# Regrouping the attention bursts inside a fused attention and SwiGLU kernel

## The chip, the core and the metric

One core of one Trainium2 chip runs the whole program. The metric is device microseconds of an execution; a profiled execution also gives a span, from its first to its last instruction, and the clock that TensorE was granted.

## The reference

Attention over 8 batches of 8 heads (576 positions, head width 64) with a band of 32 positions to each side and 8 global positions, followed by a SwiGLU feed-forward block over the 4608 tokens.

```python
scores = scale * np.matmul(q, k.transpose(0, 1, 3, 2))
mask = np.abs(pos[:, None] - pos[None, :]) <= window          # window = 32
mask = mask | is_global[:, None] | is_global[None, :]
attn = softmax(np.where(mask, scores, -1e9))
x = np.matmul(attn, v).transpose(0, 2, 1, 3).reshape(4608, 512)
g = x @ w_gate                                                # 512 x 1536
out = (g * sigmoid(g) * (x @ w_val)) @ w_out                  # 1536 x 512
```

## The kernel before

**The outer order.** The feed-forward block works on chunks of 512 tokens (`ffn`), nine of them. A chunk is 16 units: twelve gate units (`gate`, four matmuls for `pg` and four for `pv`, all 128x512, lines 754 and 784 to 793) and four output units (`outp`, twelve matmuls each, line 815). The attention of batch b is cut into steps, and the steps are put into the gaps after the units by hand: `gaps[n]` lists what follows unit n, and batch b from 2 on has the base `16 * (b - 1)`, so that it is computed during chunk b-1. Below, "gap 7" of a batch is the gap after unit 7 of that chunk. Every engine runs its instructions in program order; only waits between engines are put in by the framework.

**What a chunk needs.** Chunk c starts at token 512c, batch b at token 576b. Chunk 2 so needs the first 384 rows of batch 2, that is the outputs of `step_AV(0)`, `step_AV(1)` and `step_AV(2)`, transposed into `xT`.

**The steps of a batch from 2 on.** `step_GT` transposes the global rows. `step_S2` and `step_SG` give the scores of the two global parts (lines 444 and 422); their exponentials run on ScalarE, their masks on VectorE. `step_P2T` transposes the global weights, by TensorE for batches 2 and 3 and by a DMA on the SP queue from batch 4 on. `step_S(u)`, u from 0 to 4, gives the band scores (line 510; sixteen matmuls of 64x64, eight for u = 4), then an exponential on ScalarE (line 518) and the band mask on VectorE (line 524). `step_AV2` multiplies the global weights by the values (line 479), and three VectorE instructions turn that into `gvt` (lines 486 to 494). `step_AV(tp)`, tp from 0 to 3, and `step_AV8` add up the outputs (lines 563, 572, 591, 599) and normalise them on VectorE (lines 539 to 545). `step_X(tp)` and `step_X8` bring them into `xT` by a transposing DMA on SP.

**Buffers in PSUM.** Pool `psc` has one tile of two banks, pool `pm` another one of two banks, and pool `pf` has four single banks, which hold the `pg` and `pv` of two gate units, or an output unit's `po`. In batches 2 to 7, `step_S2`, all `step_S` and `step_AV8` use `psc`; `step_GT`, `step_SG`, `step_AV2` and all `step_AV` use `pm`.

**Loads.** Queries and keys of batches 2 to 7 are cast into DRAM by POOL's DMAs (`kf`, `qf`, line 109) and read from there by transposing DMAs on SP into `kT` and `qT` (lines 116 and 120, `tr_at`).

**The tiling of TensorE.** Profile rows carry the shape in which the array is used: gate and output matmuls and transposes 128\*128, `step_S` and the first matmuls of `step_AV` (line 563) 64\*128, `step_S2`, `step_SG` and `step_AV2` 128\*32, the other matmuls of `step_AV` and `step_AV8` 128\*64, the first two of `step_AV8` 64\*64.

Of the kernel before, what the change touches and what calls it, by code (L numbers as in the profile page):

```python
# [17 lines left out]
P = 128  # L18
# [8 lines left out]
def kernel(  # L27
# [322 lines left out]
    def attention(b):  # L350
# [122 lines left out]
            nc.scalar.copy(out=st["p2t"], in_=ps)  # L473

        def step_AV2():
            ps = mtile([P, 2, W], FP32, "ps_av2")
            for u in range(5):
                for hp in range(HP):
                    nc.tensor.matmul(  # L479
                        out=ps[32 * hp : 32 * hp + 32, :, :],  # L480
                        lhsT=st["p2t"][:, u, 32 * hp : 32 * hp + 32],
                        rhs=va[:, u, 2 * hp : 2 * hp + 2, :],
                        start=(u == 0), stop=(u == 4), skip_group_check=True,
                    )
            gv = bp.tile([P, 2, 2, W], BF16, tag="gv", name="gvt")
            nc.vector.tensor_tensor(
                out=gv, in0=bc(ps, [[0, 2], [W, 2], [1, W]]),
                in1=bc(dmh, [[2, 2], [1, 2], [0, W]]), op=ALU.mult,
            )
            lo = work.tile([P, 2, 2], FP32, tag="lo", name="lo")  # L490
            nc.vector.tensor_tensor(
                out=lo, in0=bc(ps[:, :, D : D + 1], [[0, 2], [W, 2]]), in1=dmh, op=ALU.mult
            )
            nc.vector.tensor_tensor(
                out=gv[:, :, :, D + 1], in0=lo, in1=gv[:, :, :, D], op=ALU.subtract
            )
            st["gv"] = gv

        def step_S(u):
            hg, t0 = ((0, 0), (1, 0), (0, 4), (1, 4), (None, 8))[u]  # L500
            pool, tag = (pm, "m") if (b == 0 and u in (2, 3)) or (b == 1 and u == 4) else (psc, "sc")
            ps = pool.tile([P, 2, 512], FP32, tag=tag, name="ps_s")
            if hg is None:
                slots = [(hp, hp, 8) for hp in range(HP)]
            else:
                slots = [(4 * i + tl, 2 * hg + i, t0 + tl) for i in range(2) for tl in range(4)]
            for slot, hp, t in slots:
                for par in range(2):
                    r = 64 * par
                    nc.tensor.matmul(  # L510
                        out=ps[:, par, 64 * slot : 64 * slot + 64],
                        lhsT=kT[r : r + 64, hp, 64 * t : 64 * t + P],
                        rhs=qTs[b][r : r + 64, hp, 64 * t : 64 * t + 64],
                        start=True, stop=True,
                    )
            ns = len(slots)
            pe = ppool.tile([P, 2, ns, 64], BF16, tag="pe", name="pe", bufs=3)
            nc.scalar.activation(  # L518
                out=pe, in_=ps[:, :, 0 : 64 * ns].rearrange("p r (s c) -> p r s c", c=64),
                func=AF.Exp, scale=SCALE,  # L520
            )
            pt = ppool.tile([P, 2, ns, 64], BF16, tag="p", name="pt")
            st["p", u] = pt
            mult = lambda: nc.vector.tensor_tensor(  # L524
                out=pt.rearrange("p r s c -> p (r s) c"),
                in0=pe.rearrange("p r s c -> p (r s) c"),
                in1=bc(band, [[0, 2 * ns], [1, 64]]), op=ALU.mult,
            )
            if b == 0:
                st["p*", u] = mult  # L530
            else:
                mult()
# [18 lines left out]
        def step_AV(tp):  # L551
            st["xa", tp] = work.tile([P, H, D], BF16, tag="xa", name="xa", bufs=4)
            if b == 0:
                pool, tag = (pm, "m") if tp % 2 else (psc, "sc")
            elif b < XQ:
                pool, tag = (psc, "sc") if tp == 2 else (pm, "m")
            else:
                pool, tag = pm, "m"
            full = pool.tile([P, 2, 512], FP32, tag=tag, name="ps_av")
            ps = full[:, :, 0 : 4 * W].rearrange("p g (h c) -> p g h c", c=W)  # L560
            for hg in range(2):
                r = slice(64 * hg, 64 * hg + 64)
                nc.tensor.matmul(  # L563
                    out=ps[:, hg], lhsT=st["pg"][r, P * tp : P * tp + P],
                    rhs=st["gv"][r].rearrange("p h r c -> p (h r) c"),
                    start=True, stop=False, skip_group_check=True,
                )
            for hg in range(2):
                pt = st["p", 2 * (tp // 2) + hg]
                for hl in range(4):  # L570
                    for e in range(2):
                        nc.tensor.matmul(  # L572
                            out=ps[64 * e : 64 * e + 64, hg, hl, :],
                            lhsT=pt[:, hl % 2, 4 * (hl // 2) + 2 * (tp % 2) + e, :],
                            rhs=(va if e == 0 else st["vb"])[:, tp, 4 * hg + hl, :],
                            start=False, stop=(hl == 3), skip_group_check=True,
                        )
            if b == 0:
                st["xa*", tp] = lambda: normalise(ps, st["xa", tp], 8)
            else:  # L580
                normalise(ps, st["xa", tp], 8)
# [87 lines left out]
        def vb():  # L669
            st["vb"] = load_vb(b)  # L670

        def vb0(t):
            st["vb"] = load_vb(0)
            nc.vector.tensor_copy(out=st["vb"][0:64, 0:2], in_=va[64:128, 0:2])
            nc.vector.tensor_copy(out=st["vb"][64:128, 0:2], in_=va[0:64, 1:3])
            nc.scalar.copy(out=st["vb"][0:64, 2:4], in_=va[64:128, 2:4])
            nc.scalar.copy(out=st["vb"][64:128, 2:4], in_=va[0:64, 3:5])

        L = lambda f, *a: (lambda: f(*a))
        if b == 0:  # L680
            act, dve = nc.scalar.copy, nc.vector.tensor_copy

            M = lambda *key: (lambda: st[key if len(key) > 1 else key[0]]())
            def kqm0():
                gather_mask(0, *g0, eng=nc.vector)

            return [
                L(squares), L(tables_a),
                L(step_T0, "k", 0, act), L(step_T0, "k", 1, act),
                L(step_T0, "q", 0, act), L(step_T0, "q", 1, dve), L(tables_b),  # L690
                L(step_S, 0), L(step_T0, "k", 2, dve), L(step_S, 2), L(step_T0, "k", 3, act),
                kqm0, L(step_T0, "q", 2, act), L(step_GT), L(step_T0, "q", 3, dve),
                L(step_S2), L(step_SG), M("p*", 0), M("p2*"), M("pg*"),
                L(step_S, 1), L(step_P2T), L(step_S, 3), L(warm, 1),
                M("p*", 1), L(vb0, 0), L(step_AV2), L(warm, 2), M("p*", 2),
                L(step_AV, 0), M("xa*", 0), L(step_AV, 1), L(warm, 1), M("p*", 3), L(step_X, 0),
                L(step_AV, 2), L(warm, 1), M("xa*", 1), M("xa*", 2), L(step_X, 1),
                L(step_AV, 3), M("xa*", 3),
            ], [L(step_X, 2)], [L(step_X, 3)], [L(step_S, 4), M("p*", 4)], [L(step_AV8)], [L(step_X8)]
# [17 lines left out]
        if b < XQ:  # L717
# [6 lines left out]
                14: [L(step_S, 4), L(step_AV, 3), L(step_X, 3)],  # L724
                15: [L(step_AV8)], 16: [L(step_X8)],
            }
        return {
            1: [L(step_GT), vb],
            2: [L(step_S2), L(step_SG)] + ([L(step_P2T)] if b >= XP else []),
            4: [L(step_S, 0)] + ([] if b >= XP else [L(step_P2T)]),  # L730
            7: [L(step_S, 1), L(step_AV2)],
            9: [L(step_S, 2), L(step_AV, 0), L(step_X, 0)],
            11: [L(step_S, 3), L(step_AV, 1), L(step_X, 1)],
            12: [L(step_S, 4), L(step_AV, 2), L(step_X, 2)],
            14: [L(step_AV, 3), L(step_AV8), L(step_X, 3), L(step_X8)],
        }

# [101 lines left out]
    part(1, 2 * P, 3 * P)  # L839
    part(0, 3 * P, CH)  # L840
    part(1, 3 * P, CH)
    gaps = {i: [] for i in range(9)}
    for i, g in enumerate([s4, av8, x8]):
        gaps[(0, 3, 6)[i]] += g
    def at(n, f, *a):
        gaps.setdefault(n, []).append(lambda: f(*a))

# [18 lines left out]
    for b in range(XQ, B):  # L866
        o = 16 * (b - 1)
        for i, g in attention(b).items():
            if b == 2 and i < 4:
                i += 1  # L870
            gaps[o + i] = gaps.get(o + i, []) + g
        if b > 3:
            tr_at[b] = o - 16 + 5
        if b > 4:
            cast_at[b] = o - 32 + 8
        if b > 2:
            v_at[b] = o - 16 + 2
            if b % 2 == 0:
                g_at[b] = o - 16 + 6
                m_at[b] = o - 16 + 13  # L880
# [43 lines left out]
```

The softmax here doesn't subtract the row's maximum and nothing guards it: scores larger than these inputs give would overflow.

## Time and profile before

| | |
|---|---|
| time | 360.15 us median of 3 runs (359.66 to 360.69) |
| span of the profiled execution | 361.1 us, mean granted clock 0.991 |
| TensorE matmul | 343.2 us busy, 95% |
| VectorE, ScalarE, GpSimd | 232.5, 151.2, 91.8 us busy |
| gate matmuls (line 754) | 107.1 + 107.5 us |
| output matmuls (line 815) | 92.4 us |
| band scores (line 510) | 16.2 us |
| output of attention (line 572) | 14.7 + 14.7 us |

Busy times of TensorE overlap, because matmuls are pipelined: what one costs is the distance from its start to the start of the next. A wait is charged to the engine that stood idle and named after what ended last before it resumed. Idle time of an engine other than the one that sets the end costs nothing by itself.

### The profile page before, as it was taken

What the parts mean: (1) busy time and instruction counts of PE and PEld (TensorE: products, weight loads), DVE (VectorE), ACT (ScalarE), POOL (GpSimd) and SP (SyncE); (2) the same over time, 40 slices, a digit from 0 to 9 for tenths busy, and PEclk for the clock granted to TensorE, in tenths of its full rate; (3) what the DMA queues carried; (4) which work ended last, traced back from release to release, by engine and by line L of the source; (5) the groups of instructions that cost most, each with busy time, mean ns of one, the idle gap of its engine ahead of it and who ended that gap; (6) DMA issues with size and microseconds to landing.
All of it is one profiled execution on the core that took longest, in us unless ns stands there. A gap on an engine that the chain in (4) does not pass through costs nothing.

```text
span 361.1 us, 7611 instructions
## 1 busy us (share of the span) xinstructions
PE 343.2 (95%) x3079; PEld 168.9 (47%) x3131; DVE 232.5 (64%) x468; ACT 151.2 (42%) x231; POOL 91.8 (25%) x110
## 2 busy tenths in 40 slices
PE   2989999999979999999999999999999999999996
PEld 2565554444434444444444444444444444444444
DVE  6777784388715893688458854886388727814750
ACT  5745762455313552354235532553254323323322
POOL 7964754805145111600183011000000000000000
PEclk9989999999998999999999999999999999999999
DMA  7999999999999998998989989622330230011002
GB/s 107 145 205 204 184 207 156 124 249 158 156 176 199 140 154 125 130 206 129 120 151 156 165 101 148 148 55 61 100 104 2 58 96 30 2 58 59 2 15 102
DMA packets 153539, 44.14 MB, mean 122 GB/s; under 512 B 140064, under 2 KB 148000, under 8 KB 153504
## 3 DMA queue, kind: packets, MB, share of 16 engines
q0 software_dynamic: 101216, 19.14, 67.1%
q1 hardware_dynamic: 52288, 24.51, 34.2%
q8 instruction: 24, 0.39, 0.5%
q14 instruction: 11, 0.09, 0.1%
HBM read 38.02 MB, written 16.52 MB: 151 GB/s over the span
## 4 chain that ended last, share of the span: by engine, by line
PE 84%; DMA 7%; DVE 3%; ACT 2%; issue 2%; POOL 1%; another core or an unknown queue 1%; SPq 0%; POOLq 0%; DVEq 0%
PE pg L754 24%; PE pv L754 23%; PE po L815 22%; PE ps_s L510 3%; PE ps_av L572 3%; DMA xT<-xa 2%; DMA p2t<-p 2%; DMA k_bf<-in_k_dram 2%; PE ps_av L563 1%; ACT pe L518 1%; PE ps_s L444 1%; DVE pt L524 1%; PE po L802 1%; PE ps_av L479 1%; PE ps_t L367 1%
## 5 line engine op out<-in xcount | busy, mean ns | idle before, releaser
L754 PE MATMUL pg<-xT,wg_sb 128*128 128x512 bf16 x399 | 107.1, 382 | 4.4 <-DMA xT<-xa 2.5
L754 PE MATMUL pv<-xT,wv_sb 128*128 128x512 bf16 x413 | 107.5, 382 | 0.2
L787 DVE SCALAR_TENSOR_TENSOR gv<-th,pg 128x512 bf16<-128x512 bf16 x107 | 73.4, 686 | 49.9 <-ACT th L785 49.1
L785 ACT ACTIVATE th<-pg 128x512 bf16<-128x512 f32 x107 | 63.9, 598 | 85.7 <-PE pg L754 82.9
L815 PE MATMUL po<-wo_sb,h 128*128 128x512 bf16 x399 | 92.4, 380 | 0.7
L791 DVE TENSOR_TENSOR h<-gv,pv 128x512 bf16<-128x512 bf16 x107 | 73.6, 688 | 11.8 <-PE pg L754 0.5
L754 PEld LDWEIGHTS <-wv_sb 128*128 128x128 bf16 x424 | 41.7, 98 | 50.7 <-issue 1.1
L754 PEld LDWEIGHTS <-wg_sb 128*128 128x128 bf16 x424 | 38.7, 98 | 47.0 <-issue 5.7
L815 PEld LDWEIGHTS <-h 128*128 128x128 bf16 x420 | 39.4, 98 | 45.2
L102 POOL DMA_DIRECT2D va<-in_v_dram x40 | 34.9, 976 | 91.8 <-PE ps_av L572 81.5
L820 ACT ACTIVATE osb<-po 128x512 f32<-128x512 f32 x35 | 20.9, 597 | 81.7 <-PE po L815 57.7
L518 ACT ACTIVATE pe<-ps_s 128x1024 bf16<-128x1024 f32 (+1 forms) x40 | 37.5, 938 | 17.8 <-PE ps_s L510 17.8
L524 DVE TENSOR_TENSOR pt<-pe,band 128x1024 bf16<-128x1024 bf16 (+1 forms) x40 | 25.5, 636 | 15.8 <-ACT pe L518 15.8
L545 DVE TENSOR_TENSOR xa<-ps_av,den 128x512 bf16<-128x512 f32 (+1 forms) x40 | 25.5, 638 | 1.4
L539 DVE TENSOR_REDUCE den<-ps_av 128x8 f32<-128x16 f32 (+1 forms) x40 | 6.7, 167 | 30.1 <-PE ps_av L572 27.8
L510 PEld LDWEIGHTS <-kT 64*128 64x128 bf16 x576 | 11.4, 98 | 15.9 <-issue 15.1
L109 POOL DMA_DIRECT2D kf<-in_k_dram x6 | 13.4, 2234 | 18.3 <-issue 12.6
L510 PE MATMUL ps_s<-qT,kT 64*128 64x64 bf16 x576 | 16.2, 196 | 0.1
L109 POOL DMA_DIRECT2D qf<-in_q_dram x6 | 16.0, 2659 | 1.3 <-DMA qf<-in_q_dram 1.3
L572 PE MATMUL ps_av<-vb,pt 128*64 128x66 bf16 x256 | 14.7, 201 | 0.0
L572 PE MATMUL ps_av<-va,pt 128*64 128x66 bf16 x256 | 14.7, 201 | 0.0
L572 PEld LDWEIGHTS <-pt 128*64 128x64 bf16 x512 | 11.1, 113 | 4.4 <-issue 0.5
(138 smaller groups left out, 190.2 us busy)
## 6 DMA issues: line engine op xcount, KB each, us to landing
out_dram<-osb SPq DMA_DIRECT2D x35, 256.0 KB, 2.2
vb<-va SPq DMA_DIRECT2D x14, 264.0 KB, 6.6
kf<-in_k_dram POOLq DMA_DIRECT2D x6, 576.0 KB, 17.6
qf<-in_q_dram POOLq DMA_DIRECT2D x6, 576.0 KB, 19.9
va<-in_v_dram POOLq DMA_DIRECT2D x24, 128.0 KB, 8.5
va<-in_v_dram POOLq DMA_DIRECT2D x16, 96.0 KB, 8.3
wg_sb<-in_moe_w_gate_dram POOLq DMA_DIRECT2D x3, 512.0 KB, 10.3
wv_sb<-in_moe_w_val_dram POOLq DMA_DIRECT2D x3, 512.0 KB, 12.3
```

The lines of the kernel that those rows point to most:

```text
L102: nc.gpsimd.dma_start(out=va[lo:hi, u, :, 0:D], in_=vs[t0 + lo : t0 + hi])
L109: nc.gpsimd.dma_start(out=t, in_=src[b].rearrange("h s d -> s h d"))
L510: nc.tensor.matmul(out=ps[:, par, 64 * slot : 64 * slot + 64], lhsT=kT[r : r + 64, hp, 64 * t : 64 * t + P], rhs=qTs[b][r : r + 64, hp, 64 ...
L518: nc.scalar.activation(out=pe, in_=ps[:, :, 0 : 64 * ns].rearrange("p r (s c) -> p r s c", c=64), func=AF.Exp, scale=SCALE,)
L524: mult = lambda: nc.vector.tensor_tensor(out=pt.rearrange("p r s c -> p (r s) c"), in0=pe.rearrange("p r s c -> p (r s) c"), in1=bc(band, ...
L545: nc.vector.tensor_tensor(out=xa.rearrange("p (g h) d -> p g h d", g=g), in0=bc(ps, pst + [[1, D]]), in1=bc(den, [[4, g], [1, 4], [0, D]]) ...
L572: nc.tensor.matmul(out=ps[64 * e : 64 * e + 64, hg, hl, :], lhsT=pt[:, hl % 2, 4 * (hl // 2) + 2 * (tp % 2) + e, :], rhs=(va if e == 0 els ...
L754: nc.tensor.matmul(out=ps[:, 0:n], lhsT=w[:, cc, P * fc : P * (fc + 1)], rhs=xT[:, cc, t0 : t0 + n], start=(cc == 0), stop=(cc == NCC - 1),)
L785: nc.scalar.activation(out=th[:, 0:n], in_=pg[:, 0:n], func=AF.Tanh, scale=0.5)
L787: nc.vector.scalar_tensor_tensor(out=gv[:, 0:n], in0=th[:, 0:n], scalar=1.0, in1=pg[:, 0:n], op0=ALU.add, op1=ALU.mult,)
L791: nc.vector.tensor_tensor(out=st["h"][:, fc, 0:n], in0=gv[:, 0:n], in1=pv[:, 0:n], op=ALU.mult)
L815: nc.tensor.matmul(out=po, lhsT=st["h"][:, fc, P * ts : P * (ts + 1)], rhs=wo_sb[:, fc, :], start=(fc == 0), stop=(fc == NFC - 1),)
```

## The change

For batches 3 to 7, `step_S(0)` and `step_S(1)` follow one another after unit 4, with `step_S(1)` and `step_S(2)` in `pm` instead of `psc`. `step_S(4)` moves from unit 12 to unit 7, ahead of `step_S(2)`. `step_AV2` no longer takes a tile of its own: it writes columns 256 to 387 of the first bank of the tile that `step_S(4)` wrote in columns 0 to 255. `step_AV(0)` stays after unit 9 beside `step_S(3)`; `step_AV(1)` moves after unit 12, ahead of `step_AV(2)`, which now uses `psc`. Batch 3's `step_P2T` goes after unit 5.

Batch 2 keeps its grouping, but everything is put one or two units earlier: the global steps by one, `step_AV(2)` from unit 12 to 11, the last group from unit 14 to 12.

Batch 0, which runs before the first chunk, has its shifted copies of the values on VectorE cut in two, with the second half behind `step_AV2`, and the mask of scores 2 behind the outputs 0 and 1; its last transposes move from gap 6 to gap 12. The pool of masked scores has five buffers instead of four.

```diff
         def step_AV2():
-            ps = mtile([P, 2, W], FP32, "ps_av2")
+            if b > 2:
+                ps = st["s", 4][:, 0, 256 : 256 + 2 * W].rearrange("p (r c) -> p r c", r=2)
+            else:
+                ps = mtile([P, 2, W], FP32, "ps_av2")
...
         def step_S(u):
             hg, t0 = ((0, 0), (1, 0), (0, 4), (1, 4), (None, 8))[u]
-            pool, tag = (pm, "m") if (b == 0 and u in (2, 3)) or (b == 1 and u == 4) else (psc, "sc")
+            pool, tag = (pm, "m") if (b == 0 and u in (2, 3)) or (b == 1 and u == 4) or (
+                b > 2 and u in (1, 2)
+            ) else (psc, "sc")
             ps = pool.tile([P, 2, 512], FP32, tag=tag, name="ps_s")
+            st["s", u] = ps
...
-            pt = ppool.tile([P, 2, ns, 64], BF16, tag="p", name="pt")
+            pt = ppool.tile([P, 2, ns, 64], BF16, tag="p", name="pt", bufs=5)
...
             else:
-                pool, tag = pm, "m"
+                pool, tag = (psc, "sc") if tp == 2 and b > 2 else (pm, "m")
...
+        def shift(t):
+            nc.vector.tensor_copy(out=st["vb"][0:64, t], in_=va[64:128, t])
+            nc.vector.tensor_copy(out=st["vb"][64:128, t], in_=va[0:64, t + 1])
+
         def vb0(t):
             st["vb"] = load_vb(0)
-            nc.vector.tensor_copy(out=st["vb"][0:64, 0:2], in_=va[64:128, 0:2])
-            nc.vector.tensor_copy(out=st["vb"][64:128, 0:2], in_=va[0:64, 1:3])
+            st["vb*", 0] = lambda: shift(0)
+            st["vb*", 1] = lambda: shift(1)
...
-                L(step_S, 1), L(step_P2T), L(step_S, 3), L(warm, 1),
-                M("p*", 1), L(vb0, 0), L(step_AV2), L(warm, 2), M("p*", 2),
-                L(step_AV, 0), M("xa*", 0), L(step_AV, 1), L(warm, 1), M("p*", 3), L(step_X, 0),
+                L(step_S, 1), L(step_P2T), L(step_S, 3), L(warm, 1), L(vb0, 0),
+                M("vb*", 0), M("p*", 1), L(step_AV2), M("vb*", 1), L(warm, 2),
+                L(step_AV, 0), M("xa*", 0), L(step_AV, 1), L(warm, 1), M("p*", 2), M("p*", 3), L(step_X, 0),
...
+        if b == 2:
+            return {
+                1: [L(step_GT), vb],
+                2: [L(step_S2), L(step_SG)],
+                3: [L(step_S, 0), L(step_P2T)],
+                5: [L(step_S, 1), L(step_AV2)],
+                7: [L(step_S, 2), L(step_AV, 0), L(step_X, 0)],
+                9: [L(step_S, 3), L(step_AV, 1), L(step_X, 1)],
+                11: [L(step_S, 4), L(step_AV, 2), L(step_X, 2)],
+                12: [L(step_AV, 3), L(step_AV8), L(step_X, 3), L(step_X8)],
+            }
         return {
             1: [L(step_GT), vb],
             2: [L(step_S2), L(step_SG)] + ([L(step_P2T)] if b >= XP else []),
-            4: [L(step_S, 0)] + ([] if b >= XP else [L(step_P2T)]),
-            7: [L(step_S, 1), L(step_AV2)],
-            9: [L(step_S, 2), L(step_AV, 0), L(step_X, 0)],
-            11: [L(step_S, 3), L(step_AV, 1), L(step_X, 1)],
-            12: [L(step_S, 4), L(step_AV, 2), L(step_X, 2)],
+            4: [L(step_S, 0), L(step_S, 1)],
+            5: [] if b >= XP else [L(step_P2T)],
+            7: [L(step_S, 4), L(step_S, 2), L(step_AV2)],
+            9: [L(step_S, 3), L(step_AV, 0), L(step_X, 0)],
+            12: [L(step_AV, 1), L(step_AV, 2), L(step_X, 1), L(step_X, 2)],
             14: [L(step_AV, 3), L(step_AV8), L(step_X, 3), L(step_X8)],
         }
...
-    gaps = {i: [] for i in range(9)}
+    gaps = {i: [] for i in range(13)}
     for i, g in enumerate([s4, av8, x8]):
-        gaps[(0, 3, 6)[i]] += g
+        gaps[(0, 3, 12)[i]] += g
...
         for i, g in attention(b).items():
-            if b == 2 and i < 4:
-                i += 1
             gaps[o + i] = gaps.get(o + i, []) + g
```

## The prediction

> **What bounds the kernel now.** I read the page first, then busy time by stretch, TensorE's timeline around the bursts, and last the chain of waits.
>
> ```profile
> PE 343.2 (95%) x3079; PEld 168.9 (47%) x3131; DVE 232.5 (64%) x468; ACT 151.2 (42%) x231; POOL 91.8 (25%) x110
> ...
> PE 84%; DMA 7%; DVE 3%; ACT 2%; issue 2%; POOL 1%; another core or an unknown queue 1%; SPq 0%; POOLq 0%; DVEq 0%
> ```
>
> TensorE is the bound, so only what lengthens or shortens its own line counts. Busy time by stretch (second column: length; third: TensorE) compares the chunk that carries batch 6 with one that carries no attention:
>
> ```profile
> 221.50:258.60 37.10, 36.78 (x330) 17.39 (x336) 25.54 (x50) 15.27 (x23) 0.00 (x0) 1.00 0.50 103
> ...
> 295.70:327.00 31.30, 31.17 (x143) 14.20 (x145) 16.50 (x24) 9.55 (x16) 0.00 (x0) 1.00 0.10 37
> ```
>
> Attention costs a chunk about 5.9 us. TensorE's timeline shows what that consists of:
>
> ```profile
> 230.15 1.03 PE L754 MATMUL pv<-xT,wv_sb 128*128 128x512 bf16 x4
> 231.11 0.41 PE L510 MATMUL ps_s<-qT,kT 64*128 64x64 bf16 x16
> 231.45 1.04 PE L754 MATMUL pg<-xT,wg_sb 128*128 128x512 bf16 x4
> ...
> 236.74 0.41 PE L510 MATMUL ps_s<-qT,kT 64*128 64x64 bf16 x16
> 237.07 0.47 PE L479 MATMUL ps_av<-va,p2t 128*32 128x132 bf16 x20
> 237.48 1.04 PE L754 MATMUL pg<-xT,wg_sb 128*128 128x512 bf16 x3
> ```
>
> Four gate matmuls take 0.865 from start to start, so the gates before the burst are through at 231.01; the scores start 0.10 later. Where step_AV follows step_S with the same shape, it starts 0.24 after it (241.04, 241.28); before another shape it is 0.33 or 0.34. Each change of shape so costs about 0.095. Bursts by this reading: GT 0.11, S2+SG 0.72, S(0) 0.44, S(1)+AV2 0.83, S(2)+AV(0) 0.93, S(3)+AV(1) 0.93, S(4)+AV(2) 0.80, AV(3)+AV8 1.16; sum 5.92.
>
> The only long wait of TensorE after the start is at the head of chunk 2; the chain of waits (start, length) shows it, and the stretches behind it show a price beyond the wait (last three columns: granted clock, DMA, GB/s):
>
> ```profile
> 99.18 8.89 DMA xT<-xa
> 108.07 0.04 issue
> 108.11 1.23 PE pg L754 x4
> ```
>
> ```profile
> 109.00:110.00 1.00, 1.00 (x4) 0.31 (x3) 0.00 (x0) 0.60 (x1) 0.00 (x0) 0.50 1.63 164
> 110.00:111.00 1.00, 1.00 (x4) 0.45 (x3) 0.69 (x1) 0.00 (x0) 0.00 (x0) 0.50 1.97 152
> 111.00:112.00 1.00, 0.78 (x3) 0.30 (x2) 0.69 (x1) 0.00 (x0) 0.00 (x0) 0.50 2.54 146
> ```
>
> TensorE stood idle 2.49 (105.62 to 108.11) and then ran at half clock for some 3.4 us, another 1.7. Third, batch 2's step_SG hangs on a load. Its queries' transposing DMA is issued at 62.61:
>
> ```profile
> L120 SPq DMA_TRANSPOSE qT<-qf x1: 6446/6446/6446, 62.6 to 62.6; - x1
> ...
> DMA to landing us min/median/max: 12.8/12.8/12.8
> ```
>
> It lands at 75.4, and step_SG starts at 75.47. The issue itself waited for the cast qf and kf (kf landed at 56.7), so this date belongs to the DMAs, not to TensorE.
>
> **What the skill says.** The Trainium skill, "TensorEngine Tiling (Array Packing)", section "Key Properties": "Changing tiling mode (not just tile) drains the TensorE". The trace agrees, 0.095 a change. "PSUM — Partial Sum Buffer", section "PSUM bank collisions raise a hardware error": two engines may not touch one bank in the same quarter of the partitions at once, even in other columns, and the program has to order them. No row of before shows two engines on one bank at different columns. "TensorE: Matmul & The Clock Gate", Part 1: the clock is halved after an idle window of about 3.4 us. Here 2.49 us idle was enough, and at the start the clock was 0.57 in 20 to 24 us after a stretch (16 to 20) with TensorE busy 2.22 of 4.00.
>
> **The change, part by part.** Times are differences against the profiled span, 361.1; the three runs lie 0.4 to 1.4 below it, and I put the sum on their median, 360.15.
>
> *Batches 3 to 7, shapes.* Changes of shape now: S2+SG 2, S(0) 2, S(1)+AV2 3, S(2)+AV(0) 3, S(3)+AV(1) 3, S(4)+AV(2) 3, AV(3)+AV8 5, in all 21. After: S2+SG 2, S(0)+S(1) 2, S(4)+S(2)+AV2 3, S(3)+AV(0) 3, AV(1)+AV(2) 5, AV(3)+AV8 5, in all 20. Fewer bursts save one change of shape, since step_AV changes it inside itself. In the sums: S(0)+S(1) 0.44 + 0.24 = 0.68; S(4)+S(2)+AV2 0.095 + 0.13 + 0.24 + 0.095 + 0.41 = 0.97; S(3)+AV(0) 0.93; AV(1)+AV(2) 1.27 (0.09 in, then twice 0.215 for line 563 and 0.375 for line 572, each with its change). With GT, S2+SG and AV(3)+AV8 5.84: 0.08 less a batch, 0.4 in five.
>
> *The new wait.* step_AV2 writes into a bank that the exponential of S(4) is reading, and by the page on PSUM must come after it. ScalarE starts the exponential as the scores end (236.74 + 0.41, then 237.19). S(4) has 0.29 of matmuls and its exponential 0.592 (row of 128x512 at line 518), so the exponential ends 0.92 after S(4)'s first matmul and step_AV2 starts at 0.97. Without the wait it would start at 0.13 + 0.24 + 0.095 = 0.465. TensorE stands 0.50 in every batch: all its later gates queue behind. ScalarE is free then (the tanh of unit 7 ends before the burst). Bounds: 0 if the two are not ordered, 0.6 if the change of shape comes after the wait. I take 0.50; five batches: +2.5. Batch 4 waits 0.2 for p2t in the same place already (weight load at 162.89), which the new wait swallows: -0.2.
>
> *The pair of scores.* Two exponentials (1.02 each, 0.97 apart) keep the tanh of unit 5 back to about 3.1 after the burst's start, and two masks put its gv at 3.2 to 3.9. The bank is wanted again by unit 7, 4.14 after the burst's start: hidden, with 0.2 in hand. Batch 3's step_P2T wants `pm` at 2.41, the exponential of S(1) leaves it at 2.6: +0.2, once. step_X(1) goes some 2.6 us later on SP, the issues behind it in the order as before; step_X(2) lands 4 us ahead of chunk 3 before (140.22 + 2.8 against 147.17) and goes 0.15 later: nothing. A fifth buffer of masked scores costs nothing, no engine waits for one.
>
> Together: -0.4 + 2.5 - 0.2 + 0.2 = +2.1.
>
> *Batch 2.* step_SG is now reached a unit (1.73) sooner, at about 73.4, but the queries land at 75.4: a wait of 2.0 on TensorE, with everything behind it. Unit 19 then starts at about 75.85; before, unit 20 started at 76.06. TensorE is so 1.73 - 0.21 = 1.5 later than before from there on, and ready for chunk 2 at 105.62 + 1.5 = 107.1. Batch 2's rows: SP is held by the next batch's transposes until 95.69 as before, then issues X(0), X(1) and at once X(2), at 98.5 instead of 99.18, since the store of unit 12 now comes behind it; with the 8.89 of before it lands at 107.4. Chunk 2 starts near 107.4 instead of 108.11, and does so warm: 0.7 + 1.7 = -2.4. If the wait of 2.0 halves the clock as the one of 2.49 did, 1.7 goes back: TensorE at 108.8, X(2) issued near 100.2 and landed at 109.1, against 109.8 (108.11 + 1.7) before: -0.7. I take the latter as somewhat likelier, for the start shows half clock with less idle time in one piece.
>
> *Batch 0.* On VectorE, only 0.6 of copies instead of 1.27 stand ahead of the gvt that TensorE waited 1.21 for, so up to 0.8 there, less once the chain of masks and outputs is through. It counts nothing: what is won ahead of 75.4 is given back at step_SG. The later last transposes move 0.11 of work within chunk 0: nothing.
>
> Sum: +2.1 - 0.7 = +1.4 on 360.15, rounded down for runs in which the clock stays up: 361.3.
>
> **Rivals.** (1) *The wait in batch 2 leaves the clock up* (chance 0.30): +2.1 - 2.4 = -0.3, 359.9, no measurable change. It decides where idle and work fall in the clock's window: for, 2.0 is less than 2.49; against, the start. (2) *step_AV2 does not wait* (0.17), because the two are ordered otherwise or ScalarE is earlier: -0.4 + 0.2 - 0.2 - (0.7 to 2.4), or 357.5 to 359.1, faster. Against it is that nothing else orders the two. (3) *A further stall behind the pair* (0.08): unit 7 finds its bank taken because VectorE is over the 0.2 in hand, by 0.3 to 0.5 in each batch: another 1.5 to 2.5, 363 to 364. (4) The change does what it says as to bursts; that it saves the price of a burst is what I do not believe, as the counts of shapes show. My forecast, the wait and half clock in batch 2, has 0.45.
>
> **How the numbers follow.** About 0.3%, 1.1 us, is what a measurement here can tell from no change. Slower by more: most of the forecast (0.45, a third of which falls short of 361.2) and (3), with a part of (1) where the runs of before had no half clock at 108: 0.43. Faster: (2) and a little of (1), 0.20. Same: 0.37. The range runs from the upper part of (2), 358.6, to the forecast with a wait of 0.6 and little won in batch 2, 362.6.
>
> **What would show it.** Right: step_AV2's first matmul about 0.97 after S(4)'s in batches 3 to 7, the idle time laid to the exponential of line 518; TensorE idle near 73.4 to 75.4 for qT; no wait of 2.5 at chunk 2; chunks 3 to 6 at 37.5 instead of 37.1. Wrong: chunks of 37.0, or a step_AV2 that starts 0.46 after S(4), or queries that land before 74.

## The result, and the profile after

The changed kernel takes 361.73 us (median of 4 runs, 361.55 to 362.12) against 360.27 for the one before: ratio 1.0043, 95% interval 1.0026 to 1.0061, 0.4% slower. The forecast was 361.3 and slower.

Its page has the same picture as before, TensorE busy nearly all the time:

```profile
PE 345.0 (96%) x3131; PEld 169.2 (47%) x3131; DVE 232.5 (65%) x470; ACT 150.6 (42%) x231; POOL 92.8 (26%) x110
...
PE 81%; DMA 11%; POOL 4%; DVE 1%; ACT 1%; issue 1%; POOLq 0%; DVEq 0%
```

Its span is 360.4, below the 361.1 of the profile before, although the runs say the opposite. Two spans are two single executions: the profiled execution before took 362.85 as a whole, 2.6 above the median of its runs, and the first experiment shows that it was unusual. The stretches that no disturbance reaches are comparable to a hundredth. Busy time by stretch of the changed kernel follows, for the chunks with batches 5, 6 and 7 and for the one without attention. The columns are from:to, length, busy time of TensorE, of its weight loads, of VectorE, ScalarE and GpSimd (instructions in brackets), granted clock, DMA share, GB/s; the last row is cut at 326.00, a little before the chunk's end:

```profile
182.50:219.97 37.47, 37.01 (x337) 17.56 (x336) 25.71 (x51) 15.12 (x23) 12.03 (x13) 1.00 1.27 144
219.97:257.49 37.52, 37.06 (x338) 17.63 (x337) 25.46 (x50) 15.12 (x23) 0.00 (x0) 1.00 0.49 102
257.49:295.00 37.51, 37.05 (x338) 17.60 (x337) 25.54 (x51) 15.12 (x23) 0.00 (x0) 1.00 0.25 64
295.00:326.00 31.00, 31.00 (x145) 14.11 (x144) 16.50 (x24) 9.56 (x16) 0.00 (x0) 1.00 0.11 37
```

From start to start, a chunk with attention takes 37.51 instead of 37.09. Its timeline on TensorE shows where, in gap 7:

```profile
235.41 0.52 PE L516 MATMUL ps_s<-qT,kT 64*128 64x64 bf16 x24
236.39 0.47 PE L482 MATMUL ps_s<-va,p2t 128*32 128x132 bf16 x20 [0.46 <-ACT pe L524]
236.80 1.04 PE L775 MATMUL pg<-xT,wg_sb 128*128 128x512 bf16 x4
```

The eight matmuls of scores 4 and the sixteen of scores 2 are one row here (x24). The product of `step_AV2`, now written into `ps_s`, starts 0.98 after the first of them, and the square bracket says what it waited for: 0.46 idle until ScalarE's exponential (line 524 is the old line 518). Below, "the product" is this product of `step_AV2`, and a burst is what stands in one gap. Both exponentials are one row on ScalarE:

```profile
235.75 1.51 ACT L524 ACTIVATE pe<-ps_s 128x512 bf16<-128x512 f32 x2 [0.49 <-PE ps_s L516]
```

The first of them starts at 235.75, 0.34 after the first score matmul, and with the 0.59 of its shape ends at 236.34; the product follows 0.05 later. TensorE's waits, longest in total first (total, times, longest):

```profile
PE ps_t L367 <- DMA k_bf<-in_k_dram: 5.9, 1, 5.9
PE ps_s L482 <- ACT pe L524: 2.3, 5, 0.5
PE ps_sg L422 <- DMA qT<-qf: 1.6, 1, 1.6
```

The first is the start of the program, which the kernel before has too. The second is the new wait, once in each of five batches. The third is batch 2's `step_SG`, which TensorE now reaches before its queries have landed; it starts at 75.32. The wait for `xT` at chunk 2 is gone from the list; chunk 2 starts at 107.04. The clock is full throughout.

### The profile page after: what moved, and what is told of

The parts are those of the page before. It is cut to its first block, busy times and chain, and to the rows that moved or that the text cites. A ratio compares the mean times of both kernels' runs of the same rounds, so it can differ in the third digit from the quotient of the medians.

```text
span 360.4 us, 7678 instructions
## 1 busy us (share of the span) xinstructions
PE 345.0 (96%) x3131; PEld 169.2 (47%) x3131; DVE 232.5 (65%) x470; ACT 150.6 (42%) x231; POOL 92.8 (26%) x110
## 4 chain that ended last, share of the span: by engine, by line
PE 81%; DMA 11%; POOL 4%; DVE 1%; ACT 1%; issue 1%; POOLq 0%; DVEq 0%
PE po L836 25%; PE pg L775 23%; PE pv L775 23%; DMA q_bf<-in_q_dram 3%; DMA qT<-qf 3%; PE ps_av L578 3%; DMA va<-in_v_dram 3%; PE ps_s L516 2%; DMA vb<-va 2%; POOL va L102 1%; PE ps_av L569 1%; ACT pe L524 1%; PE po L823 1%; PE ps_s L482 1%; PE ps_s L444 1%
## 5 line engine op out<-in xcount | busy, mean ns | idle before, releaser
L836 PE MATMUL po<-wo_sb,h 128*128 128x512 bf16 x420 | 94.5, 379 | 0.0
L524 ACT ACTIVATE pe<-ps_s 128x1024 bf16<-128x1024 f32 (+1 forms) x40 | 36.5, 938 | 14.4 <-PE ps_s L516 14.2
L516 PE MATMUL ps_s<-qT,kT 64*128 64x64 bf16 x576 | 14.5, 196 | 0.0
```

The lines of the kernel that those rows point to most:

```text
L516: nc.tensor.matmul(out=ps[:, par, 64 * slot : 64 * slot + 64], lhsT=kT[r : r + 64, hp, 64 * t : 64 * t + P], rhs=qTs[b][r : r + 64, hp, 64 ...
L524: nc.scalar.activation(out=pe, in_=ps[:, :, 0 : 64 * ns].rearrange("p r (s c) -> p r s c", c=64), func=AF.Exp, scale=SCALE,)
L836: nc.tensor.matmul(out=po, lhsT=st["h"][:, fc, P * ts : P * (ts + 1)], rhs=wo_sb[:, fc, :], start=(fc == 0), stop=(fc == NFC - 1),)
```

## Experiments

Each ratio is against the kernel before, in the same session; that kernel had medians of 360.52 (first four) and 359.99 (last four). Its single runs spread from 358.5 to 363.2. The intervals, in brackets behind the ratios, reach 0.2 to 0.3% to each side; the chunk lengths in a profile resolve far more.

**The kernel before, profiled again.** No edit.

> The kernel before, profiled once more. Theory: the profiled execution of before (span 361.1, half clock at 20 to 24 us and at 109 to 112 us) was a slow one of its kind; the timed runs (360.27) correspond to a span near 358.5, so this profile should show a span of 358.3 to 359.3, full clock behind the wait at chunk 2 (the 1.7 us gone) and a wait for xT there of about 2. Rival: the half clock is the rule in before, and this profile shows a span of 360.8 to 361.3 with it.

Span 359.4. The stretches behind the wait for `xT`:

```profile
109.00:110.00 1.00, 1.00 (x7) 0.44 (x5) 0.08 (x1) 0.60 (x1) 0.00 (x0) 1.00 1.89 163
110.00:111.00 1.00, 0.95 (x5) 0.45 (x5) 0.90 (x2) 0.00 (x0) 0.00 (x0) 1.00 1.72 154
111.00:112.00 1.00, 1.00 (x7) 0.50 (x6) 0.75 (x2) 0.60 (x1) 0.00 (x0) 1.00 2.33 151
```

The granted clock is 1.00 where the first profile had 0.50, after a wait of 2.35, hardly shorter than 2.49. The half clock is no fixed price of that wait; chunk 2 took 37.37 here against 39.06. The span is just above the range that I gave. Chunk 2 started at 108.23, close to the 108.11 of the first profile.

**The product one unit later.** The changed kernel with

```diff
-            7: [L(step_S, 4), L(step_S, 2), L(step_AV2)],
+            7: [L(step_S, 4), L(step_S, 2)],
+            8: [L(step_AV2)],
```

> The changed kernel with step_AV2 of batches 3 to 7 moved from gap 7 to gap 8, where the exponential of scores 4 is long done. Theory (the wait of 0.46 for that exponential is what the regrouping costs): the burst of gap 7 loses 0.46 of wait and 0.41 of product and gains 0.1 for leaving with another shape, that of gap 8 costs about 0.5; 0.4 less per batch, 2.0 in five: 359.7, that is 0.5 below before. Rival (the cost sits in queues of VectorE and ScalarE behind the pairs): no gain, and with one more burst 0.5 to 1 more than the changed kernel, 362.2 to 362.7.

360.56, ratio 1.0002 (0.9983 to 1.0020). The row of a chunk with attention, its length back at that of the kernel before:

```profile
218.89:255.98 37.09, 36.35 (x332) 17.45 (x337) 25.38 (x50) 15.01 (x23) 0.00 (x0) 1.00 0.51 103
```

```profile
234.32 0.52 PE L516 MATMUL ps_s<-qT,kT 64*128 64x64 bf16 x24
234.78 1.04 PE L776 MATMUL pg<-xT,wg_sb 128*128 128x512 bf16 x4
235.65 1.03 PE L776 MATMUL pv<-xT,wv_sb 128*128 128x512 bf16 x3
236.61 0.47 PE L482 MATMUL ps_s<-va,p2t 128*32 128x132 bf16 x20
237.01 1.04 PE L776 MATMUL pg<-xT,wg_sb 128*128 128x512 bf16 x4
```

No bracket stands at the product any more. The pairs of scores, the shared bank and the moved outputs are all still there, so they cost nothing measurable by themselves: the 0.42 a chunk is the wait, less the change of shape that this trial puts back, and the rival, a cost in the queues of VectorE and ScalarE, is out. The total did not get 0.5 below the kernel before, as I had expected from batch 2: with the wait gone and the new orders of batches 0 and 2 still in place, it is level.

**Scores 4 behind scores 2.** The changed kernel with

```diff
-            7: [L(step_S, 4), L(step_S, 2), L(step_AV2)],
+            7: [L(step_S, 2), L(step_S, 4), L(step_AV2)],
```

> The changed kernel with the order in gap 7 turned to scores 2, scores 4, product, so that the exponential of scores 4 comes behind the one of scores 2 on ScalarE. Theory: the product starts about 2.0 after the first scores instead of 0.98, the wait grows from 0.46 to about 1.5 in each of five batches, 5.3 more: 367.0. Rival (TensorE is not held by that exponential): 361.7 as the changed kernel.

367.95, ratio 1.0220 (1.0188 to 1.0253).

```profile
238.23 0.52 PE L516 MATMUL ps_s<-qT,kT 64*128 64x64 bf16 x24
240.24 0.47 PE L482 MATMUL ps_s<-va,p2t 128*32 128x132 bf16 x20 [1.49 <-ACT pe L524]
```

The product starts 2.01 after the first scores and waits 1.49; the chunk takes 38.55, 1.04 more. The same wait made three times as long costs what it should in the chunks. Five times 1.04 is 5.2; the median of the four runs is 6.2 above the changed kernel's, measured in another session, and the last 1.0 is not explained.

**Batch 2 alone.** The kernel before with the diff's entry for `b == 2` and without the `i += 1`.

> The kernel before with the earlier schedule of batch 2 and nothing else. Theory: the wait at chunk 2 (2.0 to 2.5) goes, a wait of 1.6 for the queries at step_SG comes; net gain 0.5 to 1.1: 359.2 to 359.8. Rival: the two waits cancel, 360.3; or the new wait brings the half clock, 361 to 362.

360.32, ratio 0.9997 (0.9976 to 1.0017): not told apart from no change. In its profile `step_SG` waits 0.8 for the queries, chunk 2 waits 0.3 for `xT` and starts at 107.31. The gain of 0.5 to 1.1 that I had expected does not show; the interval leaves room for up to 0.9.

**The regrouping alone.** The kernel before with the diff's edits to `step_AV2`, `step_S`, `step_AV` and the schedule for `b > 2`.

> The kernel before with the regrouping of batches 3 to 7 alone (shared banks of step_AV2, pairs of scores, fifth buffer); batches 0 to 2 as before. Theory: chunks 3 to 6 take 37.5 as in the changed kernel, the wait for xT at chunk 2 stays at 2.4: about 2.2 above before, 362.7, ratio 1.006. Rival (regrouping is free, the loss comes from batch 2 or batch 0): ratio 1.000.

362.23, ratio 1.0065 (1.0044 to 1.0087), 2.2 us. Chunks 3 to 6 take 37.51 each, as in the changed kernel. The wait for `xT` was 1.5 here.

**Batch 0 alone.** The kernel before with the diff's edits to `vb0`, the order of batch 0 and the gap of its last transposes.

> The kernel before with the reordered VectorE work of batch 0 and the later last transposes alone. Theory: what TensorE wins there is given back at the wait for xT at chunk 2, whose date the DMA queues set; chunk 2 starts at 108.1 to 108.3 as before, ratio 1.000. Rival: the 0.3 to 1 us won ahead of chunk 0 reach the end, ratio 0.997 to 0.999.

359.79, ratio 0.9987 (0.9966 to 1.0007): no effect that can be told. The wait for `xT` was 1.6, chunk 2 started at 107.07.

**Batch 2's rows by TensorE.** The kernel before with

```diff
-            if b >= XB:
+            if b >= XB and not (b == 2 and tp == 2):
                 c0 = S * b + P * tp
                 nc.sync.dma_start_transpose(
...
-            12: [L(step_S, 4), L(step_AV, 2), L(step_X, 2)],
+            12: [L(step_S, 4), L(step_AV, 2)] + ([] if b == 2 else [L(step_X, 2)]),
+            13: [L(step_X, 2)] if b == 2 else [],
```

> The kernel before, with batch 2's step_X(2) as four transposes on TensorE after unit 13 and a copy on ScalarE, as batches 0 and 1 do it, instead of the transposing DMA. Theory (that DMA's landing is the whole wait of 2.4 at chunk 2): the work costs 0.2, then batch 2's step_X(1), landed near 106.2, is the last that chunk 2 needs; chunk 2 starts at 106.1 to 106.4 instead of 108.2: 1.8 to 2.1 less, 358.5, ratio 0.9945. Rival (TensorE runs into another late transfer, for example the next queries, and gives it back): ratio 0.999 to 1.000.

358.78, ratio 0.9952 (0.9933 to 0.9971): 1.2 us faster than the kernel before, and below the changed kernel's 361.73 of another session. I had expected 1.8 to 2.1.

```profile
99.12 0.39 PE L621 MATMUL ps_x<-ident,xa 128*128 128x128 bf16 x4
99.34 1.67 PE L816 MATMUL po<-wo_sb,h 128*128 128x512 bf16 x7
...
103.11 2.76 PE L816 MATMUL po<-wo_sb,h 128*128 128x512 bf16 x12
105.71 1.03 PE L755 MATMUL pg<-xT,wg_sb 128*128 128x512 bf16 x4
```

Four transposes cost 0.22 (99.12 to 99.34), in the shape that the output matmuls have anyway, and chunk 2 follows its predecessor at once, at 105.71. The wait for `xT` went with that one transfer.

**The product in a burst of its own.** The kernel before with `step_AV2` in gap 8 instead of gap 7.

> The kernel before with step_AV2 of batches 2 to 7 moved from gap 7, behind scores 1, to a burst of its own in gap 8: the same work with one more change of shape. Theory: a change of shape costs 0.095 and a burst nothing else, so chunks 4 to 6 take 37.19 instead of 37.09. Rival (a burst has a price of its own, which fewer bursts would save): 37.25 or more.

```profile
219.11:256.31 37.20, 36.78 (x331) 17.33 (x336) 25.55 (x50) 15.22 (x23) 0.00 (x0) 1.00 0.48 103
```

One execution, 360.64. Its chunk takes 37.20 against 37.09: one more change of shape, 0.11. One more burst shows no further price.

## Why the prediction was right, and where it was not

*The new wait* (0.50 a batch, +2.5): right in mechanism, place and size. The product came 0.98 after the first scores (predicted 0.97). Without the wait it would have come at 0.465 by the prediction's sum, so it was 0.515 late; one change of shape less, 0.095, leaves 0.42, which is what the chunk grew. Taking the wait away, with one change more, moved the chunk by -0.42; lengthening it moved it by +1.04. The exponential reads columns 0 to 255 and the product writes columns 256 to 387, and the product waited all the same. Bank and tile are the same here, so these runs do not tell for which of the two the order is kept.

*The changes of shape* (20 against 21, 0.08 less a batch): right. The trial of the product alone gives 0.11 for one; the product one unit later, which has 21 again and no wait, has the 37.09 of before.

*The pair of scores* (hidden, 0.2 in hand): right; no wait for a bank of `pf` shows on TensorE. Batch 3's `step_P2T` was put at +0.2. Its chunk grew from 37.37 (second profile) to 37.92, by 0.13 more than the others, and the trace shows the predicted reason:

```profile
117.06 1.94 ACT L524 ACTIVATE pe<-ps_s 128x1024 bf16<-128x1024 f32 x2 [0.61 <-PE ps_s L516]
119.05 0.44 PE L469 MATMUL ps_p2t<-ident,p 128*128 128x128 bf16 x5
```

The pair's second exponential ends at 119.00, and the transposes start 0.05 later, where the gates before them were through at 118.93.

*Batch 4's old wait* (-0.2): an accident of the profiled execution. Its chunk took 37.27 there and 37.09 in the second profile.

*Batch 2* is where steps failed, though the -0.7 that I took is not far from the outcome. The start was right: `step_SG` waited for the queries, 1.62 instead of 2.0; TensorE came to chunk 2 at 107.04 (predicted 107.1), and found its row there (landed at 106.37, predicted 107.4). What failed is the half clock, on both sides. Behind the wait at `step_SG` it did not come, so that rival (1) named the clock rightly. But the -2.4 that this rival then gives did not come either, for it wins back a half clock of 1.7 that the second profile does not have, and a start at 108.11 that is no fixed date: other kernels with batch 2 as before started chunk 2 at 107.12, 107.07 and 107.24, and only the two profiles of the kernel before itself at 108.11 and 108.23. Where the kernel before itself starts it in most executions, no profile shows. With batch 2 moved it was 107.04, 107.22, 106.76 and 107.31. Against the other three, the changed kernel mostly moved a wait: 1.5 to 1.6 at chunk 2 became 1.62 at `step_SG`. Two wrong terms nearly cancelled in the -0.7; that 361.3 lies so close to 361.73 is in this part luck.

Behind this stands a misreading of the reference. The prediction compared the span of 361.1 with the times of the runs and found these 0.4 to 1.4 lower. But a span is 1.7 shorter than the time of the same execution, and that execution took 362.85: the runs lay 2.2 to 3.2 below it. So it was no typical execution, and what it alone had lost could not be won in the others.

*Batch 0* (nothing): agrees with the measurement, whose interval leaves room for 0.3%. That its gain is given back at the DMA dates is argued from the waits, not shown by itself.

The sum of +2.1 for batches 3 to 7 is confirmed by the regrouping alone (+2.2, interval 1.6 to 3.1). Between this and the 1.46 of the whole change the intervals overlap. Batch 2 alone, batch 0 alone and the product one unit later show no gain from the rest that can be told from nothing; whether it wins 0.7 stays open.

## What to carry to other kernels

Before a tile moves into the free columns of a bank in use, look for the last reader of that bank: free columns did not save this product from waiting, and the wait falls on the engine that sets the end if the reader runs right ahead. Count the changes of array shape and not the bursts: putting two bursts together saves only those changes that fall away between them. When one profiled execution shows a late transfer and a slowed clock, compare its time, and not its span, with the other runs, and profile it a second time before counting on winning that back.

## What the runs showed of the hardware

The half clock after a wait depends on more than its length: an idle stretch of 2.49 us was followed by 3.4 us at 0.50 in one execution, one of 2.35 and others of 1.5 to 1.6 by none. Where the stretch lies may decide it. The first two rows are from the first profile of the kernel before, the other two from its second:

```profile
105.39:108.80 3.41, 0.92 (x6) 0.42 (x5) 0.00 (x0) 0.60 (x1) 1.34 (x2) 1.00 1.44 215
108.80:112.21 3.41, 3.19 (x9) 1.21 (x9) 1.38 (x2) 0.60 (x1) 0.00 (x0) 0.50 2.12 151
103.55:106.96 3.41, 2.33 (x11) 0.88 (x9) 1.03 (x4) 0.60 (x1) 2.80 (x4) 1.00 1.59 180
106.96:110.37 3.41, 2.10 (x9) 1.07 (x11) 0.45 (x1) 0.60 (x1) 0.32 (x1) 1.00 1.47 233
```

In the first profile the clock was at half from 20.05 to 23.46 and from 108.80 to 112.21. Both stretches are 3.413 long, and they begin 88.75 apart, 26 such steps; the second begins 0.69 after TensorE had resumed. Counted in these steps from where the clock's records begin, the wait for `xT` lies whole within one step in the first profile (TensorE busy for 0.92 of it) and is cut in two by an edge at 106.96 in the second (busy for 2.33 and 2.10). This is read from the traces; no trial moved the wait against the steps. Nor does a threshold come out of them: a step with 2.01 busy was followed by half clock (product one unit later, from 20.26), one with 1.79 was not (changed kernel, from 71.99, the wait for the queries).

The product's matmuls started 0.05 after the end of the exponential that they waited for, less than the 0.095 to 0.11 of a change of shape elsewhere, so that here the change was hidden in the wait.
